# Forward and backward of a linear-attention and GLU block: transposes of h, o and gnd by DMA, gate and up tails as one chunk, and an order written out for the first tiles and the last backward tiles

## The chip, the cores and the metric

The kernel runs on one core of a Trainium2 chip. The metric is the device time of one execution in microseconds (us). The kernel before took 906.61 us (median of three runs, 905.71 to 907.32).

## The reference

One pre-LN block of linear attention and SwiGLU, with its whole backward pass. S = 2048 tokens, D = 640, H = 32 heads of 20, F = 1728, everything in bf16. The outputs are h2 and the gradients of x, wqkv, wo, w1, w3 and w2 for a given gradient of h2.

```python
def _A_ref(x, wqkv, wo):
    q, k, v = split_heads(x @ wqkv)
    phi = lambda t: jnp.where(t > 0, t + 1, jnp.exp(t)) + 1e-6
    pq, pk = phi(q), phi(k)
    kv = jnp.einsum("bhsd,bhse->bhde", pk, v)
    z = jnp.einsum("bhsd->bhd", pk)
    num = jnp.einsum("bhqd,bhde->bhqe", pq, kv)
    den = jnp.einsum("bhqd,bhd->bhq", pq, z)[..., None] + 1e-6
    return merge_heads(num / den) @ wo

def _B_ref(x, w1, w3, w2):
    gate, up = x @ w1, x @ w3
    return (_silu(gate) * up) @ w2

h  = x + _A_ref(_layernorm(x), wqkv, wo)
h2 = h + _B_ref(_layernorm(h), w1, w3, w2)
out, vjp = jax.vjp(...); return (out, *vjp(grad_out))
```

## The kernel before, in words

The program order is the order on each engine: nothing reorders it. Tokens are worked in 16 tiles of 128 (t) or 4 chunks of 512 (c); F is padded to 14 chunks of 128 (fc), the last of which holds only 64 columns. Almost all DMAs are issued from SyncE's queue (SP), plain ones by `dma` and transposing ones by `dmaT`; a few go out from ACT's. An instruction of SP that waits for its data holds up everything behind it on SP. Stages, with the us at which they stand in the profile:

1. **p1, 0 to 84** (L284 to 313). Per tile: layernorm statistics on DVE (`ln1.run`, L139 to 141), their inverse root on POOL (ln_rs, L143), xn on DVE (`p1_norm`, L146), five transposes of xn on TensorE (`p1_tr`, L214) with a copy on ACT, then k, v and for some tiles q (`p1_mm`, L220), and phi on DVE and ACT. `kv_group` (L249 to 265) sums k and v products of four tiles in a bank "big", of which v and k use the same three, and DVE adds them into kvacc (L259, L261). The weights wqkv are loaded in three pieces of 640 columns (L159), the others one by one (the list `trickle`). `zero_pads` (L270) and `make_mask` (L171) put memsets on DVE, L180 for kvbd among them, and mask operations on POOL.
2. **Prologue, 84 to 111.5** (L474). The attention outputs of the first four tiles: `f2_ndo` (o), `f2_ot` (L347: o transposed on TensorE, copied by ACT), `f2_at` (times wo, plus x: h), `f2_hn` (layernorm, hn), `f2_ht` (L393 to 403: hn transposed, copied by ACT to hnT). Both transposes share one PSUM bank, "tr".
3. **Forward chunks, 111.5 to 370** (L422 to 445, L498 to 518). For c and fc, `mlp` computes with `mm5` (five matmuls of 128x512, L408) ghh (the gradient with respect to the hidden layer), gate and up; DVE forms the hidden layer and its gradients, which are stored to hh_d and gg_d. Between them `run_side` puts the `f2_` steps of the next chunk's tiles by tables, and `o2_steps` (L447) the output matmuls of the chunk before, eight at a time.
4. **gw, 384 to 445** (L567): the gradient of w2, from hb, the transposed hidden layer (L527), loaded by DMA from hh_d. Then five transposes of a weight tail (L552), and 12 transposes that make kvbdT out of kvbd (L603).
5. **Backward loop, 448 to 601** (L749 to 800). Iteration t computes ghn(t), the gradient at hn: 54 matmuls (L633) in six parts of nine, from ggb, loaded from gg_d for two tiles at a time (L559). In between stand small steps of earlier tiles: g_h (layernorm's gradient), `b_gT` (L666: transposes it into ghT), `b_go` (L690: times wo, to gnd), `b_gndT` (L699: transposes gnd), `b_gkv` (L713), `b_gpq` (L721). Then a tail to 630 with the gradient of wo (L735).
6. **dkv phase, 630 to 676** (L874). Per tile: `dkv` (L878) and `gphi` (L721), from pkT and vaT, transposed by DMA (L811, L813), in PSUM banks "dkv" (`d_acc`, four); jobs (`grad_job`, L827, each sixteen matmuls) in banks "job" (four) stand at every second tile.
7. **e phase and the rest, 676 to 905**: the gradient of x from gT, three tiles transposed by DMA for each t (L921, L935), and the jobs that are left (960 matmuls, L827). The change leaves these as they are.

The flags TR_A and TR_B, both 0, leave the transposes of stages 3 and 5 on TensorE.

Of the kernel before, what the change touches and what calls it, by code (L numbers as in the profile page):

```python
# [28 lines left out]
TR_A, TR_B, TR_E = 0, 0, 1  # L29
# [34 lines left out]
def kernel(  # L64
# [52 lines left out]
    dma(out=x_sb[:, 1, :], in_=xS[:, 1, :])  # L117
# [40 lines left out]
    def load_wq(k):  # L158
        dma(out=wqkv[:, :, k * D:(k + 1) * D], in_=wq_v[:, :, k * D:(k + 1) * D])  # L159

    load_wq(1)
    load_wq(2)
    dma(out=x_sb[:, 2:4, :], in_=xS[:, 2:4, :])
    dma(out=x_sb[:, 4:8, :], in_=xS[:, 4:8, :])
    load_wq(0)
# [5 lines left out]
    def make_mask():  # L171
        G.memset(mask[:], 1.0)
# [7 lines left out]
        V.memset(kvbd[:], 0.0)  # L180

    w1 = U2.tile([P, DT, FP], BF16, name="w1", tag="A")
    w3 = U2.tile([P, DT, FP], BF16, name="w3", tag="B")
# [12 lines left out]
    def load_cols(dst, src, c0, c1):  # L196
        def go():
            dma(out=dst[:, c0:c1, 0:F], in_=src.rearrange("(c p) n -> p c n", p=P)[:, c0:c1, :])
        return go
# [69 lines left out]
    def zero_pads():  # L269
        for w in (w1, w3, w2T):  # L270
            V.memset(w[:, :, F:FP], 0.0)
        for v_ in va:
# [14 lines left out]
    trickle += [load_cols(w, s, c0, c1) for c0, c1 in ((0, 2), (2, 4), (4, 5))  # L287
                for w, s in ((w1, B_w1), (w3, B_w3))]
    trickle += [lambda: dma(out=wo[:], in_=A_wo.rearrange("(c p) n -> p c n", p=P))]

    for t in range(ST):
# [7 lines left out]
        if t + 1 < ST:  # L299
            p1_tr(t + 1)  # L300
        v = p1_mm(t, 2 * D)
# [6 lines left out]
        if i == 0 and g > 0:  # L308
            kv_group(g - 1, False)
# [37 lines left out]
    def f2_ot(t):  # L347
        if TR_A and t >= TPC:
# [44 lines left out]
    def f2_ht(t):  # L393
# [28 lines left out]
    def mlp(c, fc, between):  # L422
        if fc not in ghh:
            mlp_ghh(c, fc)
        gh = ghh.pop(fc)[:]
# [10 lines left out]
        V.tensor_tensor(out=gate[:], in0=gate[:], in1=sig[:], op=ALU.mult)  # L436
        V.tensor_tensor(out=s2[:], in0=gate[:], in1=s2[:], op=ALU.mult)
        V.tensor_tensor(out=sig[:], in0=s2[:], in1=sig[:], op=ALU.add)
        V.tensor_tensor(out=hhT[c][:, fc, :], in0=gate[:], in1=up[:], op=ALU.mult)
        dma(out=hh_d[f0:f0 + n, cs], in_=hhT[c][:n, fc, :])  # L440
        V.tensor_tensor(out=gate[:], in0=gate[:], in1=gh, op=ALU.mult)
        dma(out=gg_d[F + f0:F + f0 + n, cs], in_=gate[:n, :])
        V.tensor_tensor(out=sig[:], in0=sig[:], in1=up[:], op=ALU.mult)
        V.tensor_tensor(out=sig[:], in0=sig[:], in1=gh, op=ALU.mult)
        dma(out=gg_d[f0:f0 + n, cs], in_=sig[:n, :])

    def o2_steps(c, q=dma):  # L447

        jobs = [(i, j, fc) for i in range(TPC) for j in range(2) for fc in range(FT)]
        o2 = {}  # L450
        for n, (i, j, fc) in enumerate(jobs):
            if fc == 0:
                o2["ps"] = ps.tile([P, 512], F32, name="o2", bufs=2)
# [10 lines left out]
            if n % 8 == 7:  # L464
# [16 lines left out]
    mlp_ghh(0, 0)  # L481
    mlp_ghh(0, 1)
    f2_ht(3)
# [4 lines left out]
    side = ({}, {})  # L488
    for i in range(TPC):
        for k, pos, f in ((3 * i, 0, f2_ndo), (3 * i + (not TR_A), 1, f2_ot), (3 * i + 2, 1, f2_at),  # L490
                          (3 * i + 3, 0, f2_hn), (3 * i + 3 + (not TR_A), TR_A, f2_ht)):
            side[pos].setdefault(k, []).append((f, i))

    for c in range(SC):
# [3 lines left out]
        def run_side(pos, fc):  # L498
            if c + 1 < SC:
                for f, i in sorted(side[pos].get(fc, ()), key=lambda x: x[1]):  # L500
                    f((c + 1) * TPC + i)

        for fc in range(FT):
            mlp(c, fc, lambda: run_side(0, fc))
            if o2:
                next(o2)
# [23 lines left out]
    for _ in o2_steps(SC - 1, A.dma_start):  # L530
# [23 lines left out]

    ggb = {}
# [5 lines left out]
    for fc in range(FT):  # L561
# [9 lines left out]
        A.dma_start(out=out_6[fc * P:fc * P + n, :], in_=ob[:n])  # L571
        if fc == 3:
# [7 lines left out]
    w13_tail()  # L580
# [16 lines left out]

    kvbdT = br.tile([P, CT, D], BF16, name="kvbdT")

    def block_T(dst, src, cc, dcs, eng):  # L600
        tr = h1b(len(dcs))
        for i, dc in enumerate(dcs):
            T.transpose(tr[:, i, :], src[:, dc, cc * P:(cc + 1) * P], ident[:])  # L603
        cols = dst[:, cc, dcs[0] * P:(dcs[-1] + 1) * P].rearrange("p (i q) -> p i q", q=P)
        if eng is A:
            A.copy(out=cols, in_=tr[:])
        else:
            V.tensor_copy(out=cols, in_=tr[:])

    for cc, dcs in BLOCKS:  # L610
        block_T(kvbdT, kvbd, cc, dcs, A if cc % 2 else V)
# [51 lines left out]
    def by_dma(t):  # L663
        return TR_B and t < ST - 2
# [84 lines left out]
    for t in range(ST + 3):  # L749
        g = b_ghn(t) if t < ST else wog  # L750
# [7 lines left out]
        if 0 <= t - 1 < ST:  # L758
# [3 lines left out]
        if 0 <= u < ST and not by_dma(u):  # L762
            b_gT(u)
        if t == ST:
            ln_rest.pop(t - 1)()
        part()
        if w >= 0:
            if not by_dma(w):
                b_gndT(w)
            if not TR_B:  # L770
                b_gkv(w)
        part()
        if 0 <= u < ST and not TR_B:
            b_go(u)
        part()
        if t - 1 in ln_rest and t < ST:
# [3 lines left out]
        if w >= 0 and TR_B:  # L780
            b_gkv(w)
        part()
        if 0 <= u < ST and TR_B:
            b_go(u)
        if w >= 0 and not TR_B:
            b_gpq(w)
        part()
        part()
        if w >= 0 and TR_B:
            b_gpq(w)  # L790
        if 0 <= u < ST and by_dma(u):
            b_gndT(u)
        if t == ST:
            xnN = U1.tile([P, ST, D], BF16, name="xnN", tag="Q")
            for i in range(SC):
                dma(out=xnN[:, i * TPC:(i + 1) * TPC, :], in_=xS[:, i * TPC:(i + 1) * TPC, :])
        if t > ST:
            for i in range(8):
                j = (t - ST - 1) * 8 + i
                ln1.norm(xnN[:, j, :], xnN[:, j, :], j)  # L800
    for _ in wog:
        pass
# [18 lines left out]
    njob = 4  # L821
# [25 lines left out]
    gkv_b = dx.tile([P, DT, CP], BF16, name="gkv_b")  # L847
    V.memset(gkv_b[:], 0.0)
    for m, (a, b) in enumerate(M_H):
        bank, off = KV_SLOT[m]  # L850
        V.tensor_tensor(out=gkv_b[:, m, a * DA:b * DA], in0=gkv[:, bank, off:off + M_W[m]],
                        in1=mask[:, m, 0:M_W[m]], op=ALU.mult)
# [18 lines left out]
    def d_acc():  # L871
        return ps.tile([P, 512], F32, name="dkv", bufs=4)

    for t in range(ST):  # L874
# [9 lines left out]
        if i % 2:  # L884
# [26 lines left out]
    if not TR_E:  # L911
        load_hnN()
        load_block(0)
        load_block(1)
    gT = {}

    def e_T(t, k):
        if k == 0:
            gT[t] = ex.tile([P, 15, P], BF16, name="gT", bufs=3 if TR_E else 2)
# [92 lines left out]
```

## Time and profile before

| what | value |
|---|---|
| runs (us) | 905.71, 906.61, 907.32 |
| profiled execution | 907.07 us, its span 905.3 us |
| granted TensorE clock, mean | 0.994 |
| DVE busy, ACT busy | 441.7 us (49%), 366.5 us (40%) |
| DMA | 146.17 MB, mean 161 GB/s |

The profile is one execution. Its span is the time from the first to the last instruction recorded; the execution's own time has 1.8 us around it. The busy rows give each engine's time at work. The waits view gives, for an engine's line, what ended the idle time ahead of it. The windows view repeats the busy times for stretches of the span. A row of the timeline is a start, a length, an engine, a line and operation, output and inputs, a count, and in brackets the idle time before it with what ended it. Matmuls are pipelined and a row's length has the pipeline's end in it, so the price of a group is read from the start of one row to the start of the next.

### The profile page before, as it was taken

The numbers are of one execution on the slowest core, as the hardware profiler recorded it, in microseconds if no ns is written. First come the engines' busy times: TensorE is split into PE (matmuls) and PEld (weight loads), VectorE is DVE, ScalarE is ACT, GpSimd is POOL, SyncE is SP. The second block draws the span as 40 slices with busy tenths as digits, with TensorE's granted clock in tenths as the row PEclk, the third lists the DMA queues.
The fourth block names the chain that finished last, engine by engine and source line by source line (L and its number), as shares of the span: only waits on it lengthen the run. The fifth ranks groups of instructions, "written<-read, shape, count | busy, mean of one in ns | idle before, by whom it ended". The sixth has DMA issues, their size and how long they took to land.

```text
span 905.3 us, 16415 instructions
## 1 busy us (share of the span) xinstructions
PE 871.9 (96%) x6489; PEld 599.4 (66%) x6517; DVE 441.7 (49%) x1130; ACT 366.5 (40%) x690; POOL 22.4 (2%) x42
## 2 busy tenths in 40 slices
PE   5999899999999999999999999999899999999998
PEld 3777554555555555677677777777667777777776
DVE  5777688788878776400045555655331433400000
ACT  2556777756556566111122233222332333321211
POOL 4000000000000000000000000000000000000000
PEclk9999999999999999999999999999989999999999
DMA  9688483343343373799845444426999588666751
GB/s 279 189 264 256 120 253 131 105 129 124 95 127 113 110 238 112 170 241 240 223 122 146 123 122 128 126 68 177 222 241 218 114 172 163 129 148 161 177 145 37
DMA packets 304701, 146.17 MB, mean 161 GB/s; under 512 B 206064, under 2 KB 303344, under 8 KB 304624
## 3 DMA queue, kind: packets, MB, share of 16 engines
q1 hardware_dynamic: 286112, 131.92, 57.6%
q10 hardware_dynamic: 18512, 13.20, 4.9%
q8 instruction: 51, 0.84, 0.4%
q14 instruction: 26, 0.21, 0.1%
HBM read 45.20 MB, written 50.02 MB: 105 GB/s over the span
## 4 chain that ended last, share of the span: by engine, by line
PE 82%; DMA 3%; DVE 2%; ACT 2%; issue 1%; ACTq 0%; DVEq 0%; SPq 0%
PE job L827 20%; PE mm L408 19%; PE ghn L633 13%; PE gxn L935 7%; PE gw L567 7%; PE o L456 5%; PE h L690 2%; PE at L366 2%; PE gwo L735 2%; DMA hb<-hh_d 1%; DMA vaT<-va_d 1%; PE dkv L721 1%; PE h L721 1%; PE h1b L706 1%; PE nd L329 1%
## 5 line engine op out<-in xcount | busy, mean ns | idle before, releaser
L408 PE MATMUL mm<-hnT,w 128*128 128x512 bf16 x546 | 132.7, 379 | 1.7 <-ACT hnT L403 1.0
L827 PE MATMUL job<-gb,hnN 128*128 128x288 bf16 x960 | 117.8, 286 | 0.0
L827 PEld LDWEIGHTS <-hnN 128*128 128x128 bf16 x960 | 93.9, 98 | 23.7
L633 PEld LDWEIGHTS <-ggb 128*128 128x128 bf16 x864 | 82.4, 98 | 30.2 <-issue 0.5
L408 PEld LDWEIGHTS <-w 128*128 128x128 bf16 x560 | 53.8, 98 | 61.3 <-issue 1.1
L831 ACT CAST obs<-job 128x288 bf16<-128x288 f32 (+1 forms) x90 | 36.7, 407 | 136.0 <-PE job L827 82.8
L408 PE MATMUL mm<-g2T,w2T 128*128 128x512 bf16 x266 | 68.3, 379 | 0.8
L456 PE MATMUL o<-w,hhT 128*128 128x320 bf16 x448 | 67.9, 299 | 1.0 <-DVE h L461 1.0
L633 PE MATMUL ghn<-w13a,ggb 128*128 128x320 bf16 x448 | 67.8, 299 | 0.0
L935 PE MATMUL gxn<-wqT,gT 128*128 128x320 bf16 x480 | 67.5, 299 | 0.0
L220 PE MATMUL big<-wqkv,pqT 128*128 128x320 bf16 x400 | 60.8, 309 | 3.5 <-DMA wqkv<-in_A_wqkv_dram 1.6
L567 PE MATMUL gw<-g,hb 128*128 128x320 bf16 (+1 forms) x448 | 61.1, 299 | 0.6 <-DMA hb<-hh_d 0.6
L220 PEld LDWEIGHTS <-pqT 128*128 128x128 bf16 x480 | 46.8, 100 | 22.3 <-DVE kvacc L259 1.3
L633 PE MATMUL ghn<-w13b,ggb 128*128 128x320 bf16 x416 | 61.2, 299 | 0.0
L456 PEld LDWEIGHTS <-hhT 128*128 128x128 bf16 x448 | 43.8, 98 | 24.9 <-issue 1.2
L827 PEld LDWEIGHTS <-xnN 128*128 128x128 bf16 x480 | 47.4, 99 | 18.8
L935 PEld LDWEIGHTS <-gT 128*128 128x128 bf16 x480 | 47.0, 98 | 18.2
L420 ACT CAST ghh<-mm 128x512 bf16<-128x512 f32 x56 | 32.9, 587 | 63.3 <-issue 39.3
L567 PEld LDWEIGHTS <-hb 128*128 128x128 bf16 (+1 forms) x448 | 44.1, 99 | 17.7 <-DMA hb<-hh_d 1.0
L644 ACT ACTIVATE gs<-ghn 128x640 bf16<-128x640 f32 x16 | 11.3, 704 | 95.8 <-PE ghn L633 95.8
L656 ACT ACTIVATE y<-wb,s,ln_rs 128x640 bf16<-128x640 f32 x32 | 29.4, 920 | 40.9 <-DVE wb L652 40.9
L428 ACT ACTIVATE sig<-mm 128x512 bf16<-128x512 f32 x56 | 33.4, 597 | 24.9 <-PE mm L408 24.2
(128 smaller groups left out, 1146.1 us busy)
## 6 DMA issues: line engine op xcount, KB each, us to landing
ggb<-gg_d SPq DMA_DIRECT2D x8, 1728.0 KB, 9.2
hh_d<-hhT SPq DMA_DIRECT2D x52, 128.0 KB, 1.8
gg_d<-gate SPq DMA_DIRECT2D x52, 128.0 KB, 1.9
gg_d<-sig SPq DMA_DIRECT2D x52, 128.0 KB, 1.8
out_dram<-obs ACTq DMA_DIRECT2D x60, 72.0 KB, 2.5
w<-in_B_w_dram SPq DMA_DIRECT2D x4, 864.0 KB, 5.5
va_d<-va SPq DMA_DIRECT2D x4, 768.0 KB, 6.4
out_dram<-gw2o ACTq DMA_DIRECT2D x18, 160.0 KB, 4.7
```

What stands on the lines that cost most here:

```text
L220: T.matmul(acc, lhsT=pqT[:, c, t * P:(t + 1) * P], rhs=wqkv[:, c, n0:n0 + HD], start=(c == 0), stop=(c == DT - 1))
L366: T.matmul(at[:, 0:HD], lhsT=oT[t][:, c, :], rhs=wo[:, c, j * HD:(j + 1) * HD], start=(c == 0 and not on_pe), stop=(c == DT - 1))
L408: T.matmul(acc[:], lhsT=w[:, c, fc * P:(fc + 1) * P], rhs=rhs[:, c, :], start=(c == 0), stop=(c == DT - 1))
L420: A.copy(out=ghh[fc][:], in_=acc[:])
L428: A.activation(sig[:], gp[:], AF.Sigmoid)
L456: T.matmul(o2["ps"][:, 0:HD], lhsT=hhT[c][:, fc, i * P:(i + 1) * P], rhs=w2[:, fc, j * HD:(j + 1) * HD], start=(fc == 0), stop=(fc == FT - 1))
L567: T.matmul(acc[:n, j, 0:HD], lhsT=hb[b][:, t, i * P:i * P + n], rhs=g2[:, t, j * HD:(j + 1) * HD], start=(t == 0), stop=(t == ST - 1))
L633: T.matmul(acc[:, j, 0:HD], lhsT=ggb[t // 2][:, k, lo:lo + P], rhs=rhs[:, j * HD:(j + 1) * HD], start=(k == 0), stop=(k == NG - 1))
L656: A.activation(out=y[:], in_=wb[:], func=AF.Identity, bias=s[:, 3:4], scale=st.rs[:, t:t + 1])
L827: T.matmul(acc[:, 0:n], lhsT=lhs[:, t, m * P:(m + 1) * P], rhs=rhs(t), start=(t == 0), stop=(t == ST - 1))
L831: A.copy(out=ob, in_=acc[:, 0:n])
L935: T.matmul(acc[:, j, 0:HD], lhsT=gT[t][:, k, :], rhs=wqT[:, k, j * HD:(j + 1) * HD], start=(k == 0), stop=(k == 14))
```

## The change

(a) At the start wqkv comes in halves of 320 columns among the tiles of x; the pads and the memset of kvbd stand ahead of the first normalisations; `p1_tr(0)` stands before the second tile's statistics; `kv_group` stands before v. (b) w3 loses its last 64 columns, which fill w1's padding, so that one mm5 gives the tails of gate and up: four mm5 fewer. (c) For tiles 8 to 15, `f2_ot` and `f2_ht` transpose by DMA on SP; the transposes of hn left on TensorE use the banks "mm". The output matmuls stand seven or eight at a time, and in the last chunk they use other banks. (d) The kvbdT blocks stand between the gw matmuls, the weight tail before the last of them. (e) In the backward loop ghT and gndT for t < 14 come by DMA on SP. The tail after the loop is written out by hand. (f) In the dkv phase jobs use two banks and dkv six, jobs stand at listed tiles, and the loads of pkT and vaT have fewer instructions ahead of them.

The first place: DVE at the start of the program, where the third tile's xn stands. In the kernel before:

```order
13 L141 TENSOR_SCALAR ln_ve<-ln_mv 128x2
14 L271 MEMSET w_111 128x5x32
15 L271 MEMSET w_112 128x5x32
16 L271 MEMSET w2T 128x5x32
17 L273 MEMSET va_117 128x4x48
18 L274 MEMSET va_117 128x4x32
19 L273 MEMSET va_118 128x4x48
20 L274 MEMSET va_118 128x4x32
21 L180 MEMSET kvbd 128x1920
22 L146 TENSOR_SCALAR xn<-x_sb,ln_mv,ln_rs 128x640
```

In the changed kernel (its lines differ by a few):

```order
14 L286 MEMSET kvbd 128x1920
15 L144 TENSOR_SCALAR xn<-x_sb,ln_mv,ln_rs 128x640
16 L137 BN_STATS st_150<-x_sb 128x6 x2
17 L138 BN_AGGR ln_mv<-st_150 128x2
18 L137 BN_STATS st_154<-x_sb 128x6 x2
19 L138 BN_AGGR ln_mv<-st_154 128x2
20 L139 TENSOR_SCALAR ln_ve<-ln_mv 128x2
21 L144 TENSOR_SCALAR xn<-x_sb,ln_mv,ln_rs 128x640
```

The memsets between the statistics of tiles 2 and 3 and xn of tile 2 (row 22 of before, row 21 now) are gone; that of kvbd is now ahead of the second tile's xn.

The second place: SP's queue in the backward loop, two iterations. In the kernel before, with hnb, o_sb and pqb the loads of one tile each, and ggb that of two tiles' gradients:

```order
307 L618 DMA hnb<-hn_d 128x640
308 L619 DMA o_sb<-o_d 128x640
309 L623 DMA pqb<-pq_d 128x640
310 L559 DMA ggb<-gg_d 128x27x256
311 L618 DMA hnb<-hn_d 128x640
312 L619 DMA o_sb<-o_d 128x640
313 L623 DMA pqb<-pq_d 128x640
```

In the changed kernel:

```order
321 L628 DMA hnb<-hn_d 128x640
322 L629 DMA o_sb<-o_d 128x640
323 L633 DMA pqb<-pq_d 128x640
324 L581 DMA ggb<-gg_d 128x27x256
325 L679 DMA_TRANSPOSE ghT<-g_h 128x5x128
326 L712 DMA_TRANSPOSE gndT<-gnd_5280 128x6x128
327 L628 DMA hnb<-hn_d 128x640
328 L629 DMA o_sb<-o_d 128x640
329 L633 DMA pqb<-pq_d 128x640
330 L679 DMA_TRANSPOSE ghT<-g_h 128x5x128
331 L712 DMA_TRANSPOSE gndT<-gnd_5281 128x6x128
```

Each iteration has two transposes more, and every second time that of ghT stands right behind ggb.

The diff, cut to what the prediction speaks of:

```diff
+    def load_wq(a, b):
+        dma(out=wqkv[:, :, a * HD:b * HD], in_=wq_v[:, :, a * HD:b * HD])
+    load_wq(2, 3)
+    dma(out=x_sb[:, 1, :], in_=xS[:, 1, :])
+    load_wq(3, 4)
     dma(out=x_sb[:, 2:4, :], in_=xS[:, 2:4, :])
+    load_wq(4, 5)
+    load_wq(5, 6)
     dma(out=x_sb[:, 4:8, :], in_=xS[:, 4:8, :])
-    load_wq(0)
+    load_wq(0, 2)
...
+    w3 = U2.tile([P, DT, F - FL], BF16, name="w3", tag="B")
...
+    zero_pads()
     ln1.run(x_sb, 0, 1)
-    ln1.run(x_sb, 1, 2)
     p1_norm(0)
     p1_tr(0)
+    ln1.run(x_sb, 1, 2)
+    V.memset(kvbd[:], 0.0)
     p1_norm(1)
     ln1.run(x_sb, 2, 4)
-    zero_pads()
     make_mask()
...
+    trickle += [lambda: dma(out=w1[:, :, F:FP], in_=rows(B_w3)[:, :, F - FL:F])]
...
+        if i == 0 and g > 0:
+            kv_group(g - 1, False)
         v = p1_mm(t, 2 * D)
...
     def f2_ot(t):
-        if TR_A and t >= TPC:
+        if t >= 2 * TPC:
...
     def f2_ht(t):
-        if TR_A and t >= TPC:
+        if t >= 2 * TPC:
             dmaT(out=hnT[c][:, :, i * P:(i + 1) * P], in_=hn[t][:])
             return
-        tr = ps.tile([P, DT, P], BF16, name="tr", bufs=1)
+        tr = ps.tile([P, DT, P], BF16, name="trh", tag="mm", bufs=3)
...
     def mlp(c, fc, between):
-        upp = mm5(w3, fc, hnT[c])
-        A.copy(out=up[:], in_=upp[:])
         n = P if fc < FT - 1 else FL
+        if fc < FT - 1:
+            upp = mm5(w3, fc, hnT[c])
+            A.copy(out=up[:], in_=upp[:])
+        else:
+            A.copy(out=up[:n], in_=gp[n:])
+            V.memset(hhT[c][n:, fc, :], 0.0)
...
+    def kvbd_T(cc, dcs):
+        tr = ps.tile([P, len(dcs), P], BF16, name="trk", tag="gw", bufs=4)
...
+        if fc < CT:
+            kvbd_T(*BLOCKS[fc])
...
     def by_dma(t):
-        return TR_B and t < ST - 2
+        return t < ST - 2
...
-        if t % 2 == 0 and 2 <= t <= ST - 2 and t // 2 + 1 < ST // 2:
+        if t % 2 == 0 and 2 <= t <= ST - 4:
             load_gg(t // 2 + 1)
         part()
         part()
         part()
+        if t >= 1:
             ln_rest.pop(t - 1)()
             if by_dma(t - 1):
                 b_gT(t - 1)
+        if w >= 0:
             b_gkv(w)
         part()
+        if u >= 0:
             b_go(u)
+        part()
+        if w >= 0:
             b_gpq(w)
         part()
+        if u >= 0:
             b_gndT(u)
...
-    njob = 4
+    njob = 2
...
-        return ps.tile([P, 512], F32, name="dkv", bufs=4)
+        return ps.tile([P, 512], F32, name="dkv", bufs=6)
...
-        if i % 2:
+        if t in (3, 4, 5, 6, 8, 9, 10, 12):
             next(jobs, None)
```

More of the change, by code (lines that the diff above doesn't have):

```diff
@@ L269, in zero_pads @@
     def zero_pads():
-        for w in (w1, w3, w2T):
-            V.memset(w[:, :, F:FP], 0.0)
+        V.memset(w2T[:, :, F:FP], 0.0)
         for v_ in va:
@@ L505 @@
             if o2:
-                next(o2)
+                next(o2, None)
             run_side(1, fc)
@@ L596, in h1b @@
         return ps.tile([P, n, P], BF16, name="h1b", tag="h1", bufs=2)
[L598 to L611, printed above, removed]
     gkv = ps.tile([P, 2, 512], F32, name="gkv")
@@ L779, with load_x, norm_x, part @@
                 b_gT(t - 1)
-        if w >= 0 and TR_B:
+        if w >= 0:
             b_gkv(w)
         part()
-        if 0 <= u < ST and TR_B:
+        if u >= 0:
             b_go(u)
-        if w >= 0 and not TR_B:
+        part()
+        if w >= 0:
             b_gpq(w)
         part()
[L788 to L791, printed above, removed]
+        if u >= 0:
             b_gndT(u)
[L793 to L802, printed above, removed]
+    xnN = {}
+    b_load_q(ST - 1)
+    def load_x():
+        xnN[0] = U1.tile([P, ST, D], BF16, name="xnN", tag="Q")
+        for i in range(SC):
+            dma(out=xnN[0][:, i * TPC:(i + 1) * TPC, :], in_=xS[:, i * TPC:(i + 1) * TPC, :])
+    def norm_x(a, b):
+        for j in range(a, b):
+            ln1.norm(xnN[0][:, j, :], xnN[0][:, j, :], j)
+    def part(n=1):
+        for _ in range(n):
+            next(wog, None)
+    a, b, c = ST - 1, ST - 2, ST - 3
+    part()
+    ln_rest.pop(a)()
+    load_x()
+    b_gT(b)
+    part()
+    b_gkv(c)
+    part()
+    b_go(b)
+    part(2)
+    b_gpq(c)
+    part(3)
+    b_gT(a)
+    part()
+    b_go(a)
+    b_gndT(b)
+    b_gkv(b)
+    part(2)
+    b_gpq(b)
+    norm_x(0, 8)
+    part(2)
+    b_gndT(a)
+    b_gkv(a)
+    gkv_b = kvbd
+    for m, (e0, e1) in enumerate(M_H):
+        bank, off = KV_SLOT[m]
+        V.tensor_tensor(out=gkv_b[:, m, e0 * DA:e1 * DA], in0=gkv[:, bank, off:off + M_W[m]],
+                        in1=mask[:, m, 0:M_W[m]], op=ALU.mult)
+    part(2)
+    b_gpq(a)
+    norm_x(8, ST)
+    xnN = xnN[0]
+    part(20)
     br.release()
@@ L846 @@
         load_kT(c)
[L847 to L852, printed above, removed]
     ps.release()
```

135 lines of the change are left out of this document (54 added, 81 removed).

## The prediction

> **What bounds the kernel now.** I read the page first, then TensorE's waits, then the busy time by stage, then the timeline at each edit. The page's busy rows (engine, us, share, instructions):
>
> ```profile
> span 905.3 us, 16415 instructions
> PE 871.9 (96%) x6489; PEld 599.4 (66%) x6517; DVE 441.7 (49%) x1130; ACT 366.5 (40%) x690; POOL 22.4 (2%) x42
> ```
>
> TensorE bounds the kernel. Time can be won only by giving it fewer matmuls, or by ending one of its waits. The waits view, TensorE's share of it (us in total, times, longest):
>
> ```profile
> PE tr L214 <- DVE xn L146: 9.7, 2, 6.0
> PE tr L354 <- ACT hnT L403: 4.2, 5, 0.9
> PE dkv L721 <- DMA vaT<-va_d: 2.4, 1, 2.4
> PE big L220 <- DMA wqkv<-in_A_wqkv_dram: 1.6, 1, 1.6
> PE mm L408 <- ACT hnT L403: 1.0, 1, 1.0
> PE dkv L878 <- DMA pkT<-pk_d: 1.0, 1, 1.0
> PE big L220 <- DVE kvacc L259: 1.0, 1, 1.0
> PE o L456 <- DVE h L461: 1.0, 1, 1.0
> PE big L220 <- DVE kvacc L261: 0.9, 1, 0.9
> PE tr L402 <- DVE hn L146: 0.9, 3, 0.5
> ```
>
> They sum to 23.7 us and lie where the change works: start, forward chunks, dkv phase. The windows view, five stages (window, length, then PE busy and count, PEld, DVE, ACT, POOL, PEclk, DMA share, GB/s):
>
> ```profile
> 84.20:111.50 27.30, 22.81 (x188) 15.46 (x187) 18.38 (x56) 20.55 (x47) 2.21 (x4) 1.00 0.53 167
> 445.30:448.00 2.70, 1.42 (x18) 1.05 (x18) 1.31 (x6) 1.54 (x3) 0.00 (x0) 1.00 0.56 170
> 448.00:601.40 153.40, 153.40 (x1309) 115.23 (x1309) 81.21 (x188) 44.50 (x73) 0.00 (x0) 1.00 0.42 115
> 601.40:630.40 29.00, 28.22 (x246) 21.20 (x245) 15.96 (x39) 8.04 (x12) 0.00 (x0) 1.00 0.50 156
> 630.40:675.90 45.50, 40.49 (x383) 30.21 (x382) 17.25 (x42) 16.65 (x43) 0.00 (x0) 0.92 1.08 231
> ```
>
> The backward loop (448 to 601.4) has no gap: there a removed matmul is worth its full price, and any new wait costs in full. The dkv phase (630.4 to 675.9) is the worst: gaps, a DMA share of 1.08 and a clock below 1.
>
> **Start (a).** TensorE, twice DVE and once POOL:
>
> ```profile
> 18.02 0.45 PE L214 MATMUL tr<-ident,xn 128*128 128x128 bf16 x5 [3.66 <-DVE xn L146]
> 18.31 4.56 PE L220 MATMUL big<-wqkv,pqT 128*128 128x320 bf16 x20
> 22.98 2.88 PE L220 MATMUL big<-wqkv,pqT 128*128 128x320 bf16 x20
> ```
> ```profile
> 13.73 0.37 DVE L271 MEMSET w<- 128x160 uint32 x2
> 16.12 1.66 DVE L180 MEMSET kvbd<- 128x1920 uint32 x1 [0.33 <-issue]
> ```
> ```profile
> 14.48 0.80 POOL L172 MEMSET mask<- 128x840 bf16 x1
> 21.62 0.82 POOL L143 TENSOR_TENSOR ln_rs<-ln_ve,mhalf 128x2 f32<-128x2 f32 x1 [0.29 <-DVE ln_ve L141]
> ```
>
> The third tile's transpose waits 3.66 behind memsets that run from 13.73 to 17.78; the change puts them into DVE's idle time earlier. After that wait 20 matmuls took 4.56 where the next 20 took 2.88: 1.68 more goes with it. The first k no longer needs the whole 800 KB of wk, only a half at a time: I take 0.8 of the 1.6. The two waits for kvacc (1.0 + 0.9) go, since the kv group now stands before v, whose buffer no longer waits for it. Together 8.0. Given back: the next ln_rs stands behind the mask's 7 us on POOL (14.48 to about 21.4), and TensorE comes to tile 4 earlier than that lets it: an estimated 2.0. **6.0** (4.5 to 6.8, if smaller halves land no sooner, or the masks come sooner).
>
> **Prologue and chunks (b, c).** In the prologue the single "tr" bank is waited for twice 0.78 (in the 4.2) and 1.0 at its end: 2.6. Own banks for hnT end these, but the three waits for DVE's hn (0.9) stand just behind and grow: **1.5** (1 to 2.5). In chunk c=0 the same bank costs three times 0.89 (the rest of the 4.2): **2.0**, since the next ghh waits for a gate copy some 0.2 later (1 to 2.7). Tails, and the start of gw:
>
> ```profile
> 362.79 1.24 PE L408 MATMUL mm<-g2T,w2T 128*128 128x512 bf16 x5
> 363.87 2.32 PE L408 MATMUL mm<-hnT,w 128*128 128x512 bf16 x10
> 384.24 1.94 PE L567 MATMUL gw<-g,hb 128*128 128x320 bf16 x13 [0.63 <-DMA hb<-hh_d]
> ```
> ```profile
> 370.96 18.77 SPq L527 DMA_TRANSPOSE hb<-hh_d  x2
> ```
>
> Five matmuls of 512 take 363.87 - 362.79 = 1.08. One mm5 fewer in four chunks would be 4.3, but in the last chunk it brings nothing: the gw matmuls wait for hb. Its transpose is issued at 370.96, 6.0 after the last gate matmul ends (363.87 + 1.08 = 364.95), with DVE's chain and three stores between, and frees TensorE 13.3 later. Both stretches stay. So that chunk's 1.08 and the 1.0 for h (L461) turn into a longer wait there, 0.6 to about 2.0. So three tails: **3.2** (2.2 to 3.3). After the wait of 3.66, and after 1.0 and 2.39 in a row in the dkv phase, matmuls ran at half speed. A wait of 2.0 lies below both, so I count nothing, but up to 1.7 may be lost.
>
> The Trainium skill, "TensorE: Matmul & The Clock Gate", section "What's actually happening", has the clock halve after about 3.4 us of idleness in a free-running window. By it the 2.0 us cost nothing; the 3.66 row above agrees with it.
>
> **Transposes (c, e).** The loop's rows:
>
> ```profile
> 521.60 0.44 PE L673 MATMUL h1b<-ident,g_h 128*128 128x128 bf16 x5
> 521.88 1.39 PE L633 MATMUL ghn<-w13a,ggb 128*128 128x320 bf16 x9
> 523.10 0.50 PE L706 MATMUL h1b<-ident,gnd 128*128 128x128 bf16 x6
> 523.43 0.49 PE L713 MATMUL gkv<-gnd,pqb 128*128 128x147 bf16 x5
> ```
>
> Five transposes hold the stream 521.88 - 521.60 = 0.28, six 0.33. In the forward chunks eight tiles lose two groups of five: 16 x 0.28 = **4.5** (3 to 4.5; the DMA needs some 1.3 us on SP and 2.8 to land, and the tables put users 2.6 us or more behind, which is the cover). In the loop 14 x (0.28 + 0.33) = 8.5. What could be late is read from SP's timeline, where this iteration's ggb is issued, and from three landings (min, median, max us), of ggb, gT and hnb in this order:
>
> ```profile
> 525.96 0.38 SPq L559 DMA_DIRECT2D ggb<-gg_d  x1
> ```
> ```profile
> DMA to landing us min/median/max: 8.7/9.2/15.2
> ```
> ```profile
> DMA to landing us min/median/max: 2.6/2.8/5.4
> ```
> ```profile
> DMA to landing us min/median/max: 2.1/2.2/12.3
> ```
>
> gT is the nearest row for ghT and gndT: the same shape by the same queue. ghT is issued when g_h is ready, about 4.8 us into an iteration (an estimate), and used in the next one behind four parts of nine matmuls and the gkv group: 9.98 - 0.61 + 4 x 1.22 + 0.33 = 14.6 after the first one's start (9.98 is an iteration now: 64 matmuls of 320 at 0.136, eleven transposes 0.61, and 0.33 + 0.34 for the small ones of gkv and gpq). So 2.8 us alone are ample. But at six of the t it stands just behind ggb, issued 525.96 - 521.88 = 4.1 in, perhaps 4.4 now, which lands 9.2 later, at 13.6. If ghT lands half a microsecond after it, that is 14.1 against 14.6: it just fits. The 12.3 in hnb's row, of a small load issued behind two ggb, says that the queue does make it wait. I take off 0.4 for an odd late one: **8.1** (4 to 8.6).
>
> The Trainium skill, "DMA: Bandwidth & Descriptors", section "Queues, rings and completion order", says that each DMA engine consumes the descriptors of a queue in ring order. That speaks for the wait behind ggb; hnb's 12.3 agrees.
>
> **Boundary (d).** At 445.3 to 448 TensorE works 1.42 of 2.70, in short groups with copies between. The blocks move among the gw matmuls, which hide the copies. What is left is the transposes' own time, 17 x 0.056 = 0.95 at most: **1.8** (1 to 1.8).
>
> **Tail (e)** (601.4 to 630.4): 28.22 of 29.00 is busy, mostly wo jobs that stay. The written order removes the other 0.78, but the last tile's own chain becomes exposed by a similar amount: **0.3** (-1 to 1).
>
> **dkv phase (f).** TensorE at its start, steady part and break:
>
> ```profile
> 640.57 0.50 PE L721 MATMUL dkv<-gkvT,vaT 128*128 128x140 bf16 x7
> ...
> 644.74 0.50 PE L721 MATMUL dkv<-gkvT,vaT 128*128 128x140 bf16 x7
> ...
> 657.47 0.81 PE L721 MATMUL dkv<-gkvT,vaT 128*128 128x140 bf16 x7 [2.39 <-DMA vaT<-va_d]
> ...
> 658.72 4.47 PE L827 MATMUL job<-g_q,xnN 128*128 128x320 bf16 x16
> ```
>
> Two tiles and a job take 644.74 - 640.57 = 4.17. The job's sixteen matmuls are 16 x 0.136 = 2.17 (nine take 523.10 - 521.88 = 1.22 in the loop), a tile's thirteen small ones some 0.65 at about the transposes' rate: 3.5 in all. The rest, 0.7, is a wait for a dkv bank in each of eight pairs; six banks instead of four end most: 4.5. The waits of 1.0 and 2.39 go if pkT and vaT are asked for earlier: they are now issued when the loop's gkv is done, not at 626. The half-speed job goes too (4.47 against 2.17): 2.3. Together 4.5 + 3.4 + 2.3 = 10.2. Given back: jobs with two banks wait once for their copy (0.8), and the next vaT stays some 0.4 to 1 late. **8.3** (4 to 9.5).
>
> **Sum.** 6.0 + 1.5 + 2.0 + 3.2 + 4.5 + 8.1 + 1.8 + 0.3 + 8.3 = 35.7. The profiled execution took 907.07 (span 905.3 and 1.8 around it), so 871.4; the median of the runs shown, 906.61, is 0.5 lower, so **871**. The bounds sum to 19.7 and 40.6: 887 and 866. About 0.2% (1.8 us) is what a measurement of this kernel can tell from no change.
>
> **The rivals.** *Forecast* (0.65): the parts add as above.
> *ggb delays ghT* (0.18): for it, the half microsecond of room above and more traffic than before; against it, a DMA share of only 0.42 in this stage. Six even iterations waiting 1.2 us each: 871 + 7 = 878.
> *The dkv phase and the start keep their DMA waits* (0.12): the DMA share of 1.08 speaks for it, since the transposes of pkT and vaT are as many as before; earlier issue speaks against. Half of both gains goes: 871 + 7 = 878.
> *Slower* (0.03): the transposes by DMA become the loop's pace. If every ghT or gndT comes late, 14 iterations wait. The other parts give 27.6 and the removed matmuls 8.5, so it turns slower than before from 36.1 / 14 = 2.6 us each; or from 1.3 if each wait then halves the clock for about as long. At 3 us: 907 + 6 = 913. The e phase speaks against it: each of its 16 tiles has three such transposes (gT), and no wait of TensorE for gT stands in the waits view.
> *It doesn't do what it says* (0.02): the waits only move to the next buffer, the transposes' gain is eaten by them, and the time stays within 0.2%.
>
> **How the numbers follow.** The forecast's own spread and the two rivals at 878 make 865 to 884; beyond it lie all bounds failing together, the slower case and no change. Faster by over 0.2%: 0.65 + 0.18 + 0.12 = 0.95; same 0.02; slower 0.03.
>
> **What would show it.** In the changed profile: TensorE busy about 17 us less, its waits about half; no 3.66 and no 4.56 at the start; iterations of the loop 9.4 us apart, not 9.98 (a wait "h <- DMA ghT" at every second one is the rival); gw waiting for hb about 2 us; the dkv phase near 37 us with PEclk close to 1. Wrong would be: TensorE waiting for ghT, gndT, oT or hnT by several microseconds in total, or a dkv phase still above 42.

## The result, and the profile after

The changed kernel took 875.33 us (median of four runs, 873.39 to 875.57) against 906.64 for the one before, measured with it: ratio 0.9651, 95% interval 0.9634 to 0.9667. That is 31.3 us, forecast was 35.6 with a range of 865 to 884. Its profiled execution took 875.49, span 873.8.

The page's busy rows after:

```profile
span 873.8 us, 16002 instructions
PE 851.7 (97%) x6263; PEld 582.2 (67%) x6263; DVE 441.0 (50%) x1134; ACT 334.6 (38%) x643; POOL 20.4 (2%) x42
```

TensorE's busy time fell by 20 us, where the matmuls removed are worth 17 at the prediction's prices (8.5 in the loop, 4.5 in the forward chunks, 4.3 for four mm5). The other 11 us are idle time that ended. TensorE's share of the waits view after, the longest five:

```profile
PE tr L218 <- DVE xn L144: 6.2, 2, 5.6
PE job L865 <- ACT obs L869: 3.4, 1, 3.4
PE trh L407 <- DVE hn L144: 1.9, 4, 0.8
PE dkv L731 <- DMA vaT<-va_d: 1.1, 2, 0.7
PE h L700 <- DMA ghT<-g_h: 0.9, 2, 0.6
```

The second row is new. No row of before has a job waiting for obs, and the prediction has none there either. To place it, here are the stages by the start of the first matmul of each kind, from TensorE's timelines of both kernels (us from the span's start):

| from ... to the first matmul of the next | before | after | won | forecast |
|---|---|---|---|---|
| start, to late q (81.50; 73.67) | 81.5 | 73.7 | 7.8 | 6.0 |
| prologue, to ghh (106.88; 97.38) | 25.4 | 23.7 | 1.7 | 1.5 |
| chunks, to gw (384.24; 363.13) | 277.4 | 265.8 | 11.6 | 9.7 |
| gw and boundary, to ghn (448.04; 425.14) | 63.8 | 62.0 | 1.8 | 1.8 |
| loop, to gwo (601.75; 571.63) | 153.7 | 146.5 | 7.2 | 8.1 |
| tail, to the first job (630.46; 600.25) | 28.7 | 28.6 | 0.1 | 0.3 |
| dkv phase, to the k jobs (675.89; 637.85) | 45.4 | 37.6 | 7.8 | 8.3 |
| seven jobs, to gxn (691.10; 659.47) | 15.2 | 21.6 | -6.4 | 0 |
| the rest | 214.2 | 214.3 | -0.1 | 0 |

Six rows of the table are within 1 us of the forecast. Start and chunks won 3.7 more than forecast, and the seven jobs lost 6.4, for which the prediction has no term. These jobs belong to stage 7: the change leaves its code as it was, but not its time. TensorE's timeline of the changed kernel there:

```profile
637.85 4.51 PE L865 MATMUL job<-g_k,xnN 128*128 128x320 bf16 x32
...
650.06 7.39 PE L865 MATMUL job<-g_k,xnN 128*128 128x320 bf16 x32 [3.36 <-ACT obs L869]
657.29 2.34 PE L865 MATMUL job<-g_v,xnN 128*128 128x320 bf16 x16
```

It waits 3.36, and the next 32 matmuls take 657.29 - 650.06 = 7.23, where 32 need 4.34 at full clock: 2.9 more. The granted clock is 0.50 there, from 649.2 to 656.0. The timelines of SP and ACT, in order of time, lead back to the cause:

```profile
631.75 10.15 SPq L924 DMA_TRANSPOSE wqT<-in_A_wqkv_dram  x1
641.94 1.28 SPq L948 DMA_TRANSPOSE gT<-g_q  x1
...
642.39 0.42 ACT L869 CAST obs<-job 128x320 bf16<-128x320 f32 x1 [1.75 <-PE job L865]
...
646.48 1.22 SPq L948 DMA_TRANSPOSE gT<-g_q  x1
...
649.19 0.36 ACTq L870 DMA_DIRECT2D out_dram<-obs  x1
649.59 0.42 ACT L869 CAST obs<-job 128x320 bf16<-128x320 f32 x1 [6.77 <-DMA gT<-g_q]
```

ACT copies a job's result at 642.39, and issues its store only at 649.19. A completion semaphore is the counter by which a DMA tells that it has landed. In the trace the DMAs of both queues share eight of them, and this store waits for the one that gT's transpose for the tile after (the row at 646.48) holds; that transpose lands at 649.11. gT is issued behind wqT, whose row takes 10.15 on SP. Behind the store, on ACT, stands the next job's copy (the last row, which is put down to the same transpose). With two PSUM banks for jobs, TensorE stands behind that copy. The kernel before has two banks there as well, and no such wait.

### The profile page after: what moved, and what is told of

Its sections match the earlier page's. It is cut to its first block, busy times and chain, and to the rows that moved or that the text cites. A ratio compares the mean times of both kernels' runs of the same rounds, so it can differ in the third digit from the quotient of the medians.

```text
span 873.8 us, 16002 instructions
## 1 busy us (share of the span) xinstructions
PE 851.7 (97%) x6263; PEld 582.2 (67%) x6263; DVE 441.0 (50%) x1134; ACT 334.6 (38%) x643; POOL 20.4 (2%) x42
## 3 DMA queue, kind: packets, MB, share of 16 engines
q10 hardware_dynamic: 18512, 13.20, 5.1%
## 4 chain that ended last, share of the span: by engine, by line
PE 82%; DMA 4%; SPq 2%; DVE 1%; ACT 1%; issue 0%; ACTq 0%; DVEq 0%
PE mm L413 20%; PE job L865 20%; PE ghn L643 12%; PE gxn L954 7%; PE gw L589 7%; PE o L466 7%; DMA ghT<-g_h 2%; PE h L700 2%; PE gwo L745 2%; PE at L371 2%; SPq L924 1%; DMA vaT<-va_d 1%; DMA oT<-o_t 1%; PE h L731 1%; PE nd L334 1%; SPq L948 0%
## 5 line engine op out<-in xcount | busy, mean ns | idle before, releaser
L413 PE MATMUL mm<-hnT,w 128*128 128x512 bf16 x540 | 128.1, 379 | 0.9 <-ACT hnT L408 0.9
L865 PEld LDWEIGHTS <-hnN 128*128 128x128 bf16 x960 | 93.9, 98 | 23.7
L643 PE MATMUL ghn<-w13a,ggb 128*128 128x320 bf16 x448 | 65.6, 299 | 0.0
L643 PE MATMUL ghn<-w13b,ggb 128*128 128x320 bf16 x416 | 63.5, 299 | 0.0
L224 PE MATMUL big<-wqkv,pqT 128*128 128x320 bf16 x400 | 58.5, 304 | 0.8 <-ACT pqT L220 0.8
L425 ACT CAST ghh<-mm 128x512 bf16<-128x512 f32 x56 | 33.1, 591 | 66.9 <-issue 45.4
L589 PEld LDWEIGHTS <-hb 128*128 128x128 bf16 (+1 forms) x448 | 43.9, 99 | 16.3
L657 DVE SCALAR_TENSOR_TENSOR wb<-gs,xnN 128x640 f32<-128x640 bf16 x16 | 13.2, 825 | 64.8 <-ACT gs L654 64.8
L654 ACT ACTIVATE gs<-ghn 128x640 bf16<-128x640 f32 x16 | 11.2, 703 | 88.5 <-PE ghn L643 88.5
```

Source lines behind the costliest of these rows:

```text
L224: T.matmul(acc, lhsT=pqT[:, c, t * P:(t + 1) * P], rhs=wqkv[:, c, n0:n0 + HD], start=(c == 0), stop=(c == DT - 1))
L413: T.matmul(acc[:], lhsT=w[:, c, fc * P:(fc + 1) * P], rhs=rhs[:, c, :], start=(c == 0), stop=(c == DT - 1))
L425: A.copy(out=ghh[fc][:], in_=acc[:])
L589: T.matmul(acc[:n, j, 0:HD], lhsT=hb[b][:, t, i * P:i * P + n], rhs=g2[:, t, j * HD:(j + 1) * HD], start=(t == 0), stop=(t == ST - 1))
L643: T.matmul(acc[:, j, 0:HD], lhsT=ggb[t // 2][:, k, lo:lo + P], rhs=rhs[:, j * HD:(j + 1) * HD], start=(k == 0), stop=(k == NG - 1))
L865: T.matmul(acc[:, 0:n], lhsT=lhs[:, t, m * P:(m + 1) * P], rhs=rhs(t), start=(t == 0), stop=(t == ST - 1))
```

## The experiments

**Theory A**: the SP chain of transposes (pkT, vaT, wqT, gT) sets when the e phase can go on, by way of the stores and two job banks. **Rival B**: the transposes are late for the first gxn anyway, so that any freed wait only moves there. All ratios are to the kernel before, measured together with each kernel, so ratios are compared here, not medians of different rows.

| kernel | median us | ratio | 95% interval |
|---|---|---|---|
| the change | 875.33 | 0.9651 | 0.9634 to 0.9667 |
| four job banks in the e phase | 871.36 | 0.9603 | 0.9580 to 0.9626 |
| wqT earlier | 873.06 | 0.9617 | 0.9591 to 0.9643 |
| banks, wqT earlier, ggb behind ghT | 871.33 | 0.9601 | 0.9579 to 0.9623 |
| banks, ggb behind ghT | 869.66 | 0.9592 | 0.9578 to 0.9606 |
| memset of kvbd late again | 875.89 | 0.9665 | 0.9650 to 0.9681 |
| first loads as before | 877.25 | 0.9678 | 0.9659 to 0.9697 |
| forward transposes on TensorE | 880.76 | 0.9720 | 0.9704 to 0.9736 |
| dkv banks and job places as before | 878.56 | 0.9687 | 0.9672 to 0.9701 |
| before, dkv banks and job places alone | 906.61 | 0.9991 | 0.9979 to 1.0003 |
| before, loop transposes by DMA alone | 907.55 | 1.0016 | 1.0004 to 1.0028 |

**Four job banks in the e phase.**

```diff
-    njob = 2
+    njob = 4
     jobs = wq_jobs((1, 2))
```

> The changed kernel with four PSUM banks instead of two for the jobs of the e phase; nothing else. Theory A (the stores of the jobs wait for gT, which waits in SP's queue behind wqT, and with two banks TensorE waits for the copy behind those stores): the wait of 3.4 us for obs goes, and with it the half-speed stretch after it (32 matmuls in 7.39 instead of 4.34); 875.3 - 6.4 = 869 us. Rival B (the transposes themselves are late, so the wait only moves to the first gxn): the wait for obs goes, a wait for gT of about the same length stands before gxn(0), and the time is 873 us or more.

0.9603, some 4.3 us below the change, with intervals apart; 869 was expected. TensorE's timeline at the k jobs and the first gxn:

```profile
639.36 4.51 PE L865 MATMUL job<-g_k,xnN 128*128 128x320 bf16 x32
...
654.57 4.24 PE L954 MATMUL gxn<-wqT,gT 128*128 128x320 bf16 x30
```

The seven jobs take 15.21 again, as before the change, and gxn waits for nothing. Rival B falls, and theory A holds for this stage to the last tenth (6.4 expected, 21.62 - 15.21 = 6.4 found). ACT still waits 6.8 for gT in this profile; with four banks TensorE has work meanwhile. The whole gained 2 less than expected. About 1.1 of that stands in the loop, which has 1.8 of waits for ghT in this profile and took 147.6 where the change's own took 146.5; the rest is spread over the other stages.

**wqT earlier**: its transposing load stands behind `load_x`, right after the loop.

```diff
+    wqT = U1.tile([P, 15, D], BF16, name="wqT", tag="D")
...
+    dmaT(out=wqT[:], in_=A_wqkv[:, :])
...
-        if t == 7:
-            wqT = U1.tile([P, 15, D], BF16, name="wqT", tag="D")
-            dmaT(out=wqT[:], in_=A_wqkv[:, :])
```

> The changed kernel with the transposing load of wqT issued right after the backward loop, ahead of pkT and vaT, instead of at the eighth dkv tile. Theory A: gT is no longer behind wqT; the wait for obs (3.4) and its half-speed stretch (3.0) go, and so do the two waits for vaT (1.1): 868 us. Rival B (gT is slow by itself in this phase, or the stores wait for something else): the waits at the start of the e phase stay, 874 to 876 us; and if 14 us of wqT delay pkT, TensorE waits for it at the start of the dkv phase, some 5 us more.

0.9617, with 868 expected and 873.06 measured; the interval touches that of the change, so the stages carry the reading. The seven jobs are back to 655.46 - 640.25 = 15.21, so gT's place behind wqT was the cause of its lateness. But the waits in the dkv phase did not go. It took 39.7 instead of 37.6, with waits for vaT of 2.0 and for pkT of 0.9. Theory A had wqT as the cause of the waits for vaT too; this half of it is wrong. SP's timeline of the change could have shown it: wqT is issued at 631.75, behind the last vaT (628.50). What makes vaT late in this phase was not followed further.

**Before, with the dkv banks and job places alone.**

```diff
-    njob = 4
+    njob = 2
-        return ps.tile([P, 512], F32, name="dkv", bufs=4)
+        return ps.tile([P, 512], F32, name="dkv", bufs=6)
-        if i % 2:
+        if t in (3, 4, 5, 6, 8, 9, 10, 12):
```

> The kernel before with only the dkv phase's banks and job places of the change (two job banks, six dkv banks, jobs at the listed tiles). By the prediction's own step, which counted the phase's waits as gone: 906.6 - 8.3 = 898 us. Theory A (the chain of transposes pkT, vaT, wqT, gT on SP sets when the e phase can go on, and this edit doesn't move it): the dkv phase ends some 4 us earlier, but the wait for vaT stays or grows and a wait for obs appears at the start of the e phase: 903 to 906 us.

0.9991, which is 905.8 by the ratio: no change that can be told, within theory A's range and not the step's 898. Its TensorE timeline, at the first job, the k jobs and gxn:

```profile
631.05 2.34 PE L827 MATMUL job<-g_q,xnN 128*128 128x320 bf16 x16
...
669.63 4.51 PE L827 MATMUL job<-g_k,xnN 128*128 128x320 bf16 x32
...
688.96 1.25 PE L935 MATMUL gxn<-wqT,gT 128*128 128x320 bf16 x8
```

The dkv phase is 45.4 - 38.6 = 6.8 shorter, and the seven jobs take 19.3, 4.1 longer, with 3.8 of waits for obs, behind which the clock stayed at 1.00. In the profile 2.7 are left, in the medians less.

**The change, with the dkv banks and job places as before**: the same lines, the other way.

> The changed kernel with the dkv phase's banks and job places as before (four job banks, four dkv banks, jobs at every odd tile). By the prediction's step, which gave the banks 4.5 us: 880 us. Theory A (the SP chain of transposes sets when the e phase can go on; what the dkv phase gains with the new banks it loses waiting for obs at half clock): the dkv phase grows by 4 to 5 us, the wait for obs and its half-speed stretch shrink by about as much, 874 to 877 us.

878.56, 0.9687, so neither number was met. The stages say what is behind it. The rows of its timeline:

```profile
602.54 2.34 PE L865 MATMUL job<-g_q,xnN 128*128 128x320 bf16 x16
...
646.45 4.51 PE L865 MATMUL job<-g_k,xnN 128*128 128x320 bf16 x32
...
661.71 4.24 PE L954 MATMUL gxn<-wqT,gT 128*128 128x320 bf16 x30
```

From the first job to gxn it takes 59.2, the change 659.47 - 600.25 = 59.2: phase and jobs as a whole are equal, 43.9 + 15.3 against 37.6 + 21.6. That is what theory A says. But this stretch varies between executions: in three other profiles of kernels that leave it as the change has it, it takes 57.1, 58.1 and 59.8. So one pair of profiles shows equality to a microsecond or two at best. The profiles differ mostly in the loop, where waits for ghT are 2.5 here and 0.9 there and which the edit does not touch. Why the medians differ by 3 us is not settled.

**Banks, with wqT earlier and ggb behind ghT; then banks and ggb alone.**

```diff
-        if t % 2 == 0 and 2 <= t <= ST - 4:
-            load_gg(t // 2 + 1)
         part()
...
             if by_dma(t - 1):
                 b_gT(t - 1)
+        if t % 2 == 0 and 2 <= t <= ST - 4:
+            load_gg(t // 2 + 1)
```

> The changed kernel with four job banks in the e phase, wqT loaded right after the loop, and in the loop ggb's load placed behind the transpose of g_h instead of ahead of it. Theory A: the obs wait and the vaT waits go once, not twice, and the loop's two waits for ghT (0.9) go as well: 867 us. Rival B: no better than the best of the other two.

> The changed kernel with four job banks in the e phase and with ggb's load placed behind the transpose of g_h in the loop; wqT stays where the change has it. Theory A with the queue (a ghT that stands behind ggb waits for it): the loop's waits for ghT (0.9 to 1.8 us) go and nothing else moves: some 1.5 us below the four banks alone, about 870 us. Rival (ghT is late by other traffic, not by its place): the waits for ghT stay and the time is that of the four banks alone, 871.4.

With wqT earlier 0.9601, no better than the four banks alone (0.9603), as rival B has it for this run; theory A's 867 was missed, and the dkv phase of this profile takes 40.1, with waits for pkT of 1.3 and for vaT of 1.8. Without it 0.9592, 869.66 us, as expected: the lowest of the study, 5.4 us below the change by the ratios, though its interval overlaps that of the four banks alone. The landing rows of ghT, in the change and then in this kernel (min, median, max):

```profile
DMA to landing us min/median/max: 2.6/4.4/10.2
```
```profile
DMA to landing us min/median/max: 2.6/3.0/4.6
```

A ghT issued behind ggb landed up to 10.2 us after its issue; ahead of it, 4.6 at most. The loop's waits for ghT are gone and the loop takes 570.38 - 425.19 = 145.2, which is 153.7 - 14 x 0.61: the full price of the removed transposes; with wqT earlier the loop takes 145.2 too. So the wait comes from the place in the queue. The wait is small because, as the prediction worked out, the landing just about fits: in the profiles that have ggb ahead the waits are 0.5 to 2.5 us in one to five of the iterations. Behind the edit it is gndT that stands behind ggb; it lands up to 7.9 after its issue, and TensorE never waits for it.

**Before, with the loop's transposes by DMA alone** (and the order that goes with it; the old tail):

```diff
-TR_A, TR_B, TR_E = 0, 0, 1
+TR_A, TR_B, TR_E = 0, 1, 1
```

> The kernel before with only ghT and gndT of t < 14 by DMA in the loop, in the order that goes with it. By the prediction's step, 14 x 0.61 less 0.4: 906.6 - 8.1 = 898.5 us; by the loop of the changed profile (7.2 less): 899.4. Rival (every second ghT waits for ggb by more than a microsecond): waits for ghT at six of the iterations, 903 or more.

1.0016: nothing won, and the rival's reason isn't it, since ghT is waited for only once (1.5). TensorE behind the loop:

```profile
597.63 0.69 PE L673 MATMUL h1b<-ident,g_h 128*128 128x128 bf16 x5 [2.96 <-DVE g_q L725]
598.12 2.34 PE L735 MATMUL gwo<-g_h,o_sb 128*128 128x320 bf16 x8
599.72 2.96 PE L735 MATMUL gwo<-g_h,o_sb 128*128 128x320 bf16 x18
...
632.18 1.20 PE L867 MATMUL trk<-ident,gkv_b 128*128 128x128 bf16 x12 [2.55 <-DVE gkv_b L851]
...
656.94 0.81 PE L721 MATMUL dkv<-gkvT,vaT 128*128 128x140 bf16 x7 [3.73 <-DMA vaT<-va_d]
```

The loop itself ends 6.9 us sooner: from the first ghn to the end of the last, 594.17 - 447.62 = 146.6 instead of 601.47 - 448.04 = 153.4. Then the last tile's chain is exposed, with nothing to cover it: a wait of 2.96, eight matmuls in 1.6 (599.72 - 598.12 would be 1.09 at full clock), and the tail takes 33.1 instead of 29.0. In the dkv phase the mask products wait on DVE behind normalisations of x (2.55) and vaT is waited for 3.73 instead of 2.39: 48.0 instead of 45.4. The loop's 6.9 are given back as 4.1 and 2.6. The tail that the change writes out by hand is thus what the loop's gain needs: in the changed kernel the tail takes 28.6, and the mask products stand ahead of half of the normalisations there. How much of the longer wait for vaT comes from the old tail is not shown.

**Memset of kvbd late again.**

```diff
     ln1.run(x_sb, 1, 2)
-    V.memset(kvbd[:], 0.0)
     p1_norm(1)
     ln1.run(x_sb, 2, 4)
     make_mask()
+    V.memset(kvbd[:], 0.0)
```

> The changed kernel with the memset of kvbd put back where it stood, behind the statistics of tiles 2 and 3 and the start of the mask operations. Theory C (the memset both holds up the third tile's xn and slows a mask operation on POOL that runs beside it): xn waits some 1.7 us, one mask operation takes 2 us instead of 0.4, ln_rs of tiles 4 and 5 is later by as much, and TensorE cools down again: 878 to 880 us. Rival (the start is set by the loads of x and wqkv, and the memset fits anywhere): within 1 us of 875.3.

875.89, as the rival has it; theory C falls. DVE and then TensorE of this kernel:

```profile
8.48 0.89 DVE L137 BATCH_NORM_STATS2 st<-x_sb 128x6 f32<-128x320 bf16 x2 [0.50 <-DMA x_sb<-in_A_x_dram]
...
11.15 1.66 DVE L289 MEMSET kvbd<- 128x1920 uint32 x1 [0.34 <-issue]
12.72 0.26 DVE L144 TENSOR_SCALAR xn<-x_sb,ln_mv,ln_rs 128x640 bf16<-128x640 bf16 x1
```
```profile
13.20 0.44 PE L218 MATMUL tr<-ident,xn 128*128 128x128 bf16 x5
```

Tiles 2 and 3 of x are there at 8.48 (11.43 before the change), so xn is ready at 12.98 even behind the memset, before TensorE asks for it at 13.20. The mask operation that ran beside the memset took 0.81 instead of 0.37, not 2; only 0.41 of it lay beside the memset here. This edit moves the memset of kvbd alone, and with the early loads; the other memsets stay early.

**First loads as before**: the second tile of x, then wk and wv in one piece each, then tiles 2 and 3.

```diff
-    load_wq(2, 3)
     dma(out=x_sb[:, 1, :], in_=xS[:, 1, :])
-    load_wq(3, 4)
+    load_wq(2, 4)
+    load_wq(4, 6)
     dma(out=x_sb[:, 2:4, :], in_=xS[:, 2:4, :])
-    load_wq(4, 5)
-    load_wq(5, 6)
```

> The changed kernel with the first loads as before: the second tile of x, then wk and wv in one piece each, then tiles 2 and 3 of x. Theory D (at the start the loads decide as much as the memsets: tiles 2 and 3 of x land at 11.4 instead of 8.5, and the first k waits for 800 KB): first k 1.2 us later, the masks and ln_rs of tiles 4 and 5 some 2 us later, together 877.5 to 878.5 us. The prediction's step, which gave the halves 0.8 us and the memsets the rest: 876 us.

877.25. TensorE's timeline, the transposes of tiles 2 and 3:

```profile
14.44 0.45 PE L216 MATMUL tr<-ident,xn 128*128 128x128 bf16 x5 [0.90 <-DVE xn L144]
...
18.53 0.45 PE L216 MATMUL tr<-ident,xn 128*128 128x128 bf16 x5 [0.93 <-DVE xn L144]
```

p1 ends at 75.2 instead of 73.7: the order of the first loads is worth 1.5, between theory D and the prediction. The first k comes at 7.17, as in the change (7.11), so in this profile the halves bring it nothing; in the three others with the loads as before it waits 0.94 to 1.70 for wqkv, and with halves never. What the new order does is let the tiles of x land earlier. The third tile's transpose waits 0.90 here, where the kernel before with the same loads has 3.66: most of the start's gain (81.5 - 75.2 = 6.3 of 7.8) does not need the new loads.

**Forward transposes on TensorE** for all tiles, by the table of the first chunk.

```diff
-        if t >= 2 * TPC:
+        if t >= ST:
...
-    sides = [sides(0), sides(1), sides(1)]
+    sides = [sides(0), sides(0), sides(0)]
```

> The changed kernel with the transposes of o and hn back on TensorE for all tiles, by the first chunk's table for all chunks. By the prediction's price, 16 groups of 0.28 come back and the two waits for oT (0.7) go: 879 to 880 us. Rival (the DMA transposes take as much from the rest of the queue as they give): below 877.

880.76, a little above the 879 to 880 expected; the rival's 877 falls. The chunks take 366.75 - 97.40 = 269.4, which is 3.6 more than the change: sixteen groups less the two waits for oT of 0.7. The rest of the profile's difference of 4.1 lies in the dkv phase (38.2 instead of 37.6). The medians differ by 5.4, which the profile does not explain. The wait for obs is 4.6 where the change has 3.4, and yet the seven jobs take 21.6 in both: behind it the clock was low for only 3.4 us instead of 6.8.

## Why the prediction was right, and where it was not

**Bound and direction**: right. TensorE bounds both kernels, and what was removed from its stream was won in the stages without gaps. That the total came within 4.3 us of the forecast is in part luck: start and chunks won 3.7 more than their terms, mostly for reasons that the prediction does not give, and cover more than half of the 6.4 that it overlooked. (Its upper bounds sum to 40.7, not 40.6; nothing hangs on it.)

**Transposes, boundary**: right, and close in size. The loop's 14 x 0.61 are all there once ggb is out of the way (145.2); with ggb ahead 7.2 are left of 8.1 foreseen. The queue's rival was real, in the place and by the mechanism named, but with waits of 0.9 instead of 7 us (0.5 to 2.5 in the other profiles). The forward transposes measured 3.6 against 4.5, the difference being the waits for oT, about which the prediction only said that cover of 2.6 us was there. The boundary gave 1.8.

**dkv phase**: the step that failed. The phase itself won 7.8 of the 8.3; the sum ended its look there. "Given back: jobs with two banks wait once for their copy (0.8)" was the right kind of wait, priced for the wrong copy: the one that counted stood at the start of the e phase, behind a store on ACT that waits for gT, behind wqT on SP. The chain of transposes did not get shorter with the phase: from the first pkT to wqT SP takes 663.45 - 626.33 = 37.1 before and 631.75 - 592.49 = 39.3 after, and it starts only 3.6 earlier against the phase's first job (7.8 ahead instead of 4.1). So wqT, and gT behind it, come 1.5 us earlier against the phase's first job (31.5 instead of 33.0 behind it), while TensorE comes 7.8 earlier: 6.3 are missing, and 6.4 were lost. The prediction noted that TensorE never waits for gT in the kernel before. That holds for gxn (four banks show it), but it overlooked that jobs ahead of gxn depend on gT by way of ACT. The two experiments that move banks and job places alone show the same: what the phase wins, the jobs behind it lose in large part.

**Start**: 7.8 instead of 6.0, and the reasons only in part. The prediction gave the mask on POOL 7 us and charged 2.0 for it at tile 4 (tiles counted from 0). In the changed kernel the mask takes 4.7 (11.92 to 16.66), tile 4 waits for nothing and tile 3 for 0.60. One mask operation before, and the same after, from POOL's timelines:

```profile
15.79 2.40 POOL L178 TENSOR_SCALAR_AFFINE_SELECT mask<-mask 128x147 bf16<-128x147 bf16 x1
```
```profile
13.23 0.37 POOL L179 TENSOR_SCALAR_AFFINE_SELECT mask<-mask 128x147 bf16<-128x147 bf16 x1
```

The mask's extra 2.0 us were in this single row, and they belong to the memset of kvbd beside it. In all four profiles in which such an operation is under way when that memset runs (three with the old start, and the memset late again), it ends 0.40 to 0.41 after the memset does, about its own length. The change itself moves the memset away from the mask, and the prediction kept the 7 us. The prediction gave the halves 0.8 for the first k; there they end the wait for the load, 0.8 to 1.7 with the loads as before, and the new order brings 1.5 through x. The memsets as the main cause of the 3.66 fit the run with the first loads as before, which keeps them early (0.90 left); no run moves them all back alone. With the early loads that of kvbd may stand where it stood.

**Chunks**: 11.6 instead of 9.7. The prediction counted nothing for the last chunk, since hb would land 13.3 after its issue. TensorE's timeline of the changed kernel:

```profile
345.78 14.39 PE L466 MATMUL o<-w,hhT 128*128 128x320 bf16 x104
359.73 3.56 PE L466 MATMUL o<-w,hhT 128*128 128x320 bf16 x25
363.13 4.51 PE L589 MATMUL gw<-g,hb 128*128 128x320 bf16 x32
```
```profile
351.75 18.57 SPq L541 DMA_TRANSPOSE hb<-hh_d  x2
```

hb is issued 6.0 after the last gate matmul, as foreseen, but TensorE needs it 11.4 later and does not wait. "Both stretches stay" failed in its second half: the first hb landed 10.7 after its issue, and 10.5 to 11.2 in all nine profiles with the new forward code, against 13.2, 13.7 and 14.1 in the three with the old (waits for hb of 0.63, 1.12 and 1.47). So this is no scatter from one execution to the next, and it isn't the forward transposes either, since the run that has them back on TensorE shows 11.0. The wait of 2.0 at half speed that the range provided for did not arise. Why hb lands sooner was not tried; the room left is 0.2 to 0.8 us.

**Tail**: 0.1 against 0.3 looks like a harmless term. The loop's transposes without that tail (1.0016) show that it carries most of the 6.7 us that the loop would give back: 4.1 in the tail itself, and the wait for the mask products in the dkv phase. The prediction added terms that hold only together; the sum was right because the change has them all.

## What to carry to other kernels

When a phase gets shorter on the bounding engine, put the queues that feed the next phase on the same clock: a chain of transposes that keeps its length turns the gain into a wait one phase later, and the way to it can lead over a store on a third engine. A buffer more for the engine that waits behind that store can be the cheapest answer; here two more PSUM banks (0.9603) were worth at least as much as moving the load (0.9617, with overlapping intervals). And test a part alone before calling its neighbour free: the loop's gain was nothing without the tail.

## What the hardware showed that was not expected

A store on ACT's queue was issued 6.4 us after its data was ready (642.81 to 649.19), held by a transpose on SP's queue with which it shares no data, by a completion semaphore that both queues use.

TensorE's clock dropped after waits of 3.36 (32 matmuls in 7.2 instead of 4.3) and of 2.96 (eight in 1.6 instead of 1.1). The length of a wait alone did not decide it. These windows stand right behind waits of 3.36 (the change), 2.45 (dkv banks as before), 3.40 (before, dkv banks alone) and 3.52 (first loads as before), in this order; the third number from the end is the granted clock:

```profile
650.10:655.10 5.00, 5.00 (x20) 2.73 (x20) 0.00 (x0) 0.85 (x2) 0.00 (x0) 0.50 0.83 176
629.40:632.20 2.80, 2.80 (x19) 2.11 (x20) 0.89 (x2) 0.75 (x2) 0.00 (x0) 0.50 1.16 316
681.90:686.90 5.00, 4.60 (x33) 3.20 (x33) 0.00 (x0) 0.85 (x2) 0.00 (x0) 1.00 0.83 177
654.40:659.40 5.00, 4.68 (x34) 3.23 (x34) 0.00 (x0) 0.85 (x2) 0.00 (x0) 1.00 0.81 174
```

A wait of 2.55 (the loop's transposes alone) left the clock at 1.00 too. So in these runs a wait of 2.4 to 3.5 us was in some cases followed by 3.4 or 6.8 us at half speed and in others by none, and what decides it is not shown. The Trainium skill, "TensorE: Matmul & The Clock Gate", section "What's actually happening", names an idle window of about 3.4 us: here shorter waits were enough.

A memset on DVE held up an operation of POOL on other data: a mask operation of 0.37 took 2.40 beside the memset of kvbd, and ended 0.40 after it.

A transpose of 128x640 by DMA landed 2.6 us after its issue when the queue was free.
